# ScalarE writes one column into both PSUM banks of a projection ahead of its products, in batches 2 to 4

## Chip, cores and metric

The kernel runs on one core of one Trainium2 chip. A time is device microseconds (us) of one execution of the whole program; the kernel before takes 903.56 us (median of three runs, 902.72 to 904.33). The engines are PE (TensorE, matmuls) with its weight loads (PEld), DVE (VectorE), ACT (ScalarE), POOL (GpSimd) and SP (SyncE, which issues the transfers).

## What is computed

Four batches of a linear attention with random features, then two feed-forward blocks over all 2304 rows. Cut to what matters here:

```python
def phi(x):                                    # x: (4, 8, 576, 64), omega: (128, 64)
    proj = np.einsum('bhsd,md->bhsm', x, omega)
    sq = np.sum(x * x, axis=-1, keepdims=True) / 2.0
    h = proj - sq
    h = h - np.max(h, axis=-1, keepdims=True)
    return np.exp(h) / np.sqrt(m)
q_p, k_p = phi(q * scale), phi(k * scale)
kv = einsum('bhsm,bhsd->bhmd', k_p, v)         # and z = sum of k_p over s
out = einsum('bhsm,bhmd->bhsd', q_p, kv) / (einsum('bhsm,bhm->bhs', q_p, z)[..., None] + 1e-06)
h = x @ w_in;  x = (h * np.clip(h + 3.0, 0.0, 6.0) / 6.0) @ w_out      # block 1
h = x @ w2_in; y = (h / (1.0 + np.exp(-1.702 * h))) @ w2_out           # block 2
```

## The kernel before

**Stages.** The attention of batch 1 (`b` = 0 in the code) comes first, up to about 54 us of the profile. Then block 1 runs batch by batch over 16 chunks each (`emit_h`, `emit_o`), and the attention of the next batch (`b` = 1, 2, 3) is worked off step by step between its matmuls (`side`): the span from 54 to about 410 us. From there on block 1 of the last batch and block 2 (`h_pair`, `o_pair`) run without any attention. Chunks of `emit_o` follow those of `emit_h` two units later (`LAG`).

**The projection.** `PJ(h)` projects k and q of one head (512 of the 576 rows), `PL()` the remaining 64 rows of all heads of a batch. Both call `project` (lines 282 to 291): eight products of a 64-row stationary operand with omega (64 x 128), four for each half of the partitions. The half from partition 64 on writes the bank `ps[1]`, the other the bank `ps[0]`, and they alternate, `half` = 1 first. Each product is two matmul instructions in the profile, so a projection is 16. `behind(last)` fixes the order of the eight products among themselves, not that nothing else comes between them. `features` (lines 293 to 300) then takes the maximum of each bank on DVE (L295) and four exponentials of it on ACT (L297). A batch has 8 `PJ` and one `PL`; the three batches of the change have 27 projections.

**Banks.** PSUM has eight banks. Four belong to the pool `psp`, four to `acc`. From 54 us on `bank` hands out `psp` alone, because `emit_o` (L555) accumulates in the four of `acc`. The four of `psp` go round among the products of `emit_h` (L513), read by ACT L524 and DVE L525, the projections (two at a time), KV products (L347, L355), transposes (L369, L324, L433) and the numerators (L386).

**Order.** The program is laid out by a planner that runs through the text with a simulated clock. It gives every engine a fixed list of instructions; among those whose operands and bank are free by its reckoning, the one that stands earlier in the text goes first. A `behind(x)` block adds to an instruction only that it stands after `x` in the list of the same engine. On the chip each engine goes through its list in order and waits where a semaphore is not there yet. Banks are handed out in the order of the text.

**Lines the change and the steps touch:** L289 projection matmul; L295 maximum; L297 exponentials; L363 copy of the KV product; L374 copy of the transposed features; L524, L525, L529, L530 the gate of block 1; L213, L236, L252 conversion of weights and their sums; L513, L555, L856, L1008 the matmuls of the blocks.

Of the kernel before, what the change touches and what calls it, by code (L numbers as in the profile page):

```python
# [22 lines left out]
def performer_moe_kernel(  # L23
# [13 lines left out]
    nc = tc.nc  # L37
# [50 lines left out]
    three = const.tile([P, 1], F32, name="three")  # L88
# [20 lines left out]
    def bank(shape, name):  # L109
        n_ps[0] += 1  # L110
        if banks[0] == "acc" or banks[0] == "both" and n_ps[0] % 2:
            return acc.tile(shape, F32, tag="acc", name="acc")
        return psp.tile(shape, F32, tag="ps", name="ps")

    def behind(*ins):
        stack = ExitStack()
        for i in ins:
            if i is not None:
                stack.enter_context(tc.issue_after(i.ins))
        return stack  # L120
# [158 lines left out]
        nc.scalar.copy(hi, ps)  # L279
        nc.vector.tensor_tensor(out=lo, in0=ps, in1=hi.bitcast(F32), op=ALU.subtract)  # L280

    def project(a, ps):

        last = None
        for n in range(4):
            for half in (1, 0):
                rows = HALVES[half]
                with behind(last):
                    last = nc.tensor.matmul(  # L289
                        out=ps[half][:, n, :], lhsT=a(rows, n), rhs=omt[rows, :], start=True, stop=True  # L290
                    )

    def features(ps, e):
        mx = at.tile([P, 4], F32, tag="mx", bufs=4, name="mx")
        dve = nc.vector.reduce_max(mx, ps, axis=AX.X, negate=True)  # L295
        for r in range(4):
            act = nc.scalar.activation(  # L297
                out=e[:, r, :], in_=ps[:, r, :], func=AF.Exp, bias=mx[:, r:r + 1]
            )
        return act, dve  # L300

    class Att:
# [10 lines left out]
        def PL(self):  # L313
            a, self.vl = lqkv.pop(self.b)
            self.el = at.tile([P, 2 * NPAIR, M], F32, tag="el", name="el")
            ps = [bank([P, NPAIR, M], "ps") for _ in HALVES]
            project(lambda rows, i: a[rows, i, :], ps)
            for j, p in enumerate(ps):
                features(p, self.el[:, j * NPAIR:(j + 1) * NPAIR])

# [9 lines left out]
        def PJ(self, h):  # L330
            a = qkv[self.b, h // 2][0][:, h % 2]
            ps = [bank([P, R, M], "ps") for _ in HALVES]
            project(lambda rows, n: a[rows, n // 2, n % 2, :], ps)
            self.e[h] = at.tile([P, 2, R, M], F32, tag="e", bufs=2, name="e")
            for half, p in enumerate(ps):
                self.feat[h] = features(p, self.e[h][:, half])
# [347 lines left out]
    ps = bank([P, 4, P], "ps")  # L684
# [122 lines left out]
    for u in range(len(units) + LAG):  # L807
        while fetches and fetches[0][0] <= u + AHEAD:
            fetch_w(0, *fetches.pop(0)[1:])
        if u < len(units):  # L810
            n, c = units[u]
# [433 lines left out]
```

## Time and profile before

| | |
|---|---|
| median of three runs | 903.56 us |
| the profiled execution | 906.58 us |
| its span, first to last instruction | 904.8 us |
| mean granted TensorE clock | 0.998 of full speed |
| PE busy / weight loads busy | 98% / 84% of the span |
| DVE / ACT / POOL busy | 61% / 53% / 36% |
| instructions | 16525 |

Times in the rows are those of the profiled execution, from its first instruction on. Matmuls are pipelined: a matmul is shown with a duration longer than the distance to the next one, so the distance between two starts tells what it costs PE. A view by stretches gives busy time of each engine, the granted clock and the share of the transfer engines. A timeline merges neighbours of one line into one row, with their count; the number in brackets is idle time of the engine before the row, and what ended it.

### The profile page before, as it was taken

The numbers are of one execution on the slowest core, as the hardware profiler recorded it, in microseconds if no ns is written. First come the engines' busy times: TensorE is split into PE (matmuls) and PEld (weight loads), VectorE is DVE, ScalarE is ACT, GpSimd is POOL, SyncE is SP. The second block draws the span as 40 slices with busy tenths as digits, with TensorE's granted clock in tenths as the row PEclk, the third lists the DMA queues.
The fourth block names the chain that finished last, engine by engine and source line by source line (L and its number), as shares of the span: only waits on it lengthen the run. The fifth ranks groups of instructions, "written<-read, shape, count | busy, mean of one in ns | idle before, by whom it ended". The sixth has DMA issues, their size and how long they took to land.

```text
span 904.8 us, 16525 instructions
## 1 busy us (share of the span) xinstructions
PE 886.0 (98%) x6344; PEld 757.1 (84%) x6344; DVE 554.3 (61%) x952; ACT 478.0 (53%) x973; POOL 322.6 (36%) x257
## 2 busy tenths in 40 slices
PE   8899999999999999999999999999999999999998
PEld 6667777788788778878888888878999888899998
DVE  5887688473754736475573343666887343368785
ACT  5887677376664666656553343444545232245452
POOL 0122222044636565475673121877000243440000
PEclk9999999999999999999999999999999999999999
DMA  6677669698888987778857325999889644565562
GB/s 209 226 248 270 234 239 316 245 329 282 286 275 288 342 304 290 233 276 288 314 204 256 128 98 206 349 400 356 277 288 354 233 170 162 180 174 153 158 204 82
DMA packets 74416, 224.57 MB, mean 248 GB/s; under 512 B 7521, under 2 KB 13793, under 8 KB 74337
## 3 DMA queue, kind: packets, MB, share of 16 engines
q1 hardware_dynamic: 73872, 223.12, 71.1%
q8 instruction: 50, 0.82, 0.4%
q10 hardware_dynamic: 464, 0.39, 0.2%
q14 instruction: 30, 0.24, 0.1%
HBM read 160.57 MB, written 62.91 MB: 247 GB/s over the span
## 4 chain that ended last, share of the span: by engine, by line
PE 82%; DVE 8%; ACT 6%; issue 1%; POOL 1%; DMA 1%; DVEq 0%; SPq 0%; ACTq 0%; POOLq 0%
PE o L1008 19%; PE o L555 18%; PE ps L513 18%; PE h L856 16%; PE hl L873 3%; PE ps L289 2%; ACT e L297 2%; DVE w L236 2%; PE ps L386 1%; PE ps L347 1%; ACT wtop L213 1%; DVE mx L295 1%; DVE wtop L221 1%; PE ps L369 1%; DVE gs L530 1%
## 5 line engine op out<-in xcount | busy, mean ns | idle before, releaser
L513 PE MATMUL ps<-x,wss 128*128 128x512 f32 x768 | 195.5, 399 | 2.5 <-ACT el L297 1.1
L1008 PE MATMUL o<-wss,gs 128*128 128x256 f32 x1512 | 173.9, 277 | 0.2 <-DVE gs L977 0.2
L1008 PEld LDWEIGHTS o<-wss,gs 128*128 128x128 f32 x1512 | 173.4, 188 | 0.9 <-DVE gs L977 0.6
L513 PEld LDWEIGHTS ps<-x,wss 128*128 128x128 f32 x768 | 140.9, 189 | 35.0 <-ACT wss L239 3.1
L856 PE MATMUL h<-xo,wss 128*128 128x512 f32 x672 | 158.5, 391 | 0.9 <-DVE t L889 0.9
L856 PEld LDWEIGHTS h<-xo,wss 128*128 128x128 f32 x672 | 123.9, 188 | 27.5 <-DVE t L889 1.8
L228 POOL TENSOR_TENSOR w<-w,wpow 128x1024 f32<-128x1024 f32 x32 | 69.2, 2162 | 204.6 <-DVE wpow L225 166.7
L525 DVE SCALAR_TENSOR_TENSOR ga<-ga,ps 128x512 f32<-128x512 f32 x80 | 50.1, 632 | 121.1 <-ACT ga L524 121.1
L899 POOL TENSOR_TENSOR g<-g,c 128x512 f32<-128x512 f32 x48 | 64.7, 1349 | 164.0 <-ACT g L898 163.8
L976 ACT CAST gs<-g 128x512 fp32r<-128x512 f32 x112 | 69.6, 622 | 80.3 <-PE o L1008 49.3
L555 PE MATMUL o<-gs,wsh 128*128 128x512 f32 (+1 forms) x480 | 110.4, 374 | 1.2 <-ACT gs L529 1.0
L555 PE MATMUL o<-gs,wss 128*128 128x512 f32 (+1 forms) x480 | 109.5, 374 | 0.2 <-ACT gs L529 0.2
L253 POOL TENSOR_TENSOR wsn<-w,wsn 128x512 fp32r<-128x512 f32 x64 | 86.6, 1367 | 63.5 <-ACT wsn L252 63.5
L977 DVE TENSOR_TENSOR gs<-g,gs 128x512 fp32r<-128x512 f32 x112 | 79.9, 716 | 33.6 <-ACT gs L976 32.3
L524 ACT ACTIVATE ga<-ps,three 128x512 f32<-128x512 f32 x80 | 51.4, 650 | 86.5 <-PE ps L513 86.0
L555 PEld LDWEIGHTS o<-gs,wsh 128*128 128x128 f32 x480 | 82.2, 188 | 17.6 <-ACT gs L529 1.4
L555 PEld LDWEIGHTS o<-gs,wss 128*128 128x128 f32 x480 | 82.4, 188 | 15.8 <-ACT gs L529 0.4
L297 ACT ACTIVATE e<-ps,mx 128x128 f32<-128x128 f32 x220 | 61.1, 396 | 23.5 <-DVE mx L295 23.3
L530 DVE TENSOR_TENSOR gs<-ga,gs 128x512 fp32r<-128x512 f32 x80 | 62.5, 791 | 16.5 <-ACT gs L529 14.7
L898 ACT ACTIVATE g<-c 128x512 f32<-128x512 f32 x48 | 30.3, 632 | 60.2 <-DVE c L889 60.2
L529 ACT CAST gs<-ga 128x512 fp32r<-128x512 f32 x80 | 46.0, 580 | 27.8 <-DVE ga L525 27.4
L252 ACT CAST wsn<-w 128x512 fp32r<-128x512 f32 x64 | 38.3, 620 | 39.5 <-DVE w L236 13.2
(132 smaller groups left out, 1102.7 us busy)
## 6 DMA issues: line engine op xcount, KB each, us to landing
wss<-left SPq DMA_DIRECT2D x56, 512.0 KB, 3.9
wss<-ws0i SPq DMA_DIRECT2D x48, 512.0 KB, 4.9
wraw<-in_w_in_dram SPq DMA_DIRECT2D x32, 512.0 KB, 5.4
wraw<-in_w_out_dram SPq DMA_DIRECT2D x32, 512.0 KB, 6.3
left<-wsn SPq DMA_DIRECT2D x32, 512.0 KB, 3.7
wss<-ws0o SPq DMA_DIRECT2D x24, 512.0 KB, 4.6
ws0i<-wss SPq DMA_DIRECT2D x16, 512.0 KB, 3.3
wss<-sumsa SPq DMA_DIRECT2D x16, 512.0 KB, 3.5
```

The lines of the kernel that those rows point to most:

```text
L228: nc.gpsimd.tensor_tensor(out=w, in0=w, in1=q, op=ALU.mult)
L253: nc.gpsimd.tensor_tensor(out=s[:, :, 1], in0=t, in1=s[:, :, 0].bitcast(F32), op=ALU.subtract)
L297: act = nc.scalar.activation(out=e[:, r, :], in_=ps[:, r, :], func=AF.Exp, bias=mx[:, r:r + 1])
L513: nc.tensor.matmul(out=ps, lhsT=w[:, wi, kk, :], rhs=x[:, xi, kk, :], start=(m == 0), stop=(m == 3 * NK - 1),)
L524: nc.scalar.activation(out=g, in_=ps, func=AF.Relu, bias=three)
L530: gate[1] = nc.vector.tensor_tensor(out=s[:, 1, :], in0=g, in1=s[:, 0, :].bitcast(F32), op=ALU.subtract)
L555: nc.tensor.matmul(out=ps[:, e, :], lhsT=w[:, wi, cols], rhs=s[:, gi, :], start=(c == 0 and m == 0 and e == 0), stop=(c == NC - 1 and m == ...
L856: nc.tensor.matmul(out=ps, lhsT=s[:, wi, q, :], rhs=xop[q, op][:, xi], start=(first and m == 0), stop=(m == 5), skip_group_check=not first,)
L899: mul = eng.tensor_tensor(out=g, in0=g, in1=src, op=ALU.mult)
L976: split_ins[0] = nc.scalar.copy(hi, g)
L977: split_ins[1] = nc.vector.tensor_tensor(out=lo, in0=g, in1=hi.bitcast(F32), op=ALU.subtract)
L1008: last_row[0] = nc.tensor.matmul(out=out, lhsT=s[:, gi, d * P:(d + 1) * P], rhs=w[:, wi, :], start=(start and m == 0), stop=(stop and m == 2),
```

## The change

In batches 2 to 4 (`self.b > 0`) a projection begins with two copies on ACT: the constant column `three` (128 x 1) into the first column of `ps[0]`, then into that of `ps[1]`. Both columns are overwritten by the products. A product of either half writes the bank that its copy wrote and so follows it; as `half` = 1 comes first, and its copy stands second, the first product follows both. Of batch 1 nothing is changed.

```diff
-    def project(a, ps):
+    def project(a, ps, both=False):
 
         last = None
+        if both:
+            with behind(nc.scalar.copy(ps[0][:, 0, 0:1], three)):
+                nc.scalar.copy(ps[1][:, 0, 0:1], three)
         for n in range(4):
             for half in (1, 0):
                 rows = HALVES[half]
...
-            project(lambda rows, i: a[rows, i, :], ps)
+            project(lambda rows, i: a[rows, i, :], ps, self.b > 0)
...
-            project(lambda rows, n: a[rows, n // 2, n % 2, :], ps)
+            project(lambda rows, n: a[rows, n // 2, n % 2, :], ps, self.b > 0)
```

## Rows read from the trace of the kernel before

**Rows 1.** The page: busy us (share of the span) and instructions of each engine.

```profile
PE 886.0 (98%) x6344; PEld 757.1 (84%) x6344; DVE 554.3 (61%) x952; ACT 478.0 (53%) x973; POOL 322.6 (36%) x257
```

**Rows 2.** Busy time by stretch: length, then engines (x instructions), clock, transfers.

```profile
54.00:410.00 356.00, 351.90 (x2609) 279.05 (x2608) 223.07 (x405) 230.35 (x491) 152.64 (x118) 1.00 0.79 278
410.00:905.00 495.00, 489.58 (x3185) 443.62 (x3184) 292.76 (x456) 210.27 (x374) 161.78 (x128) 1.00 0.67 228
```

**Rows 3.** Waits of PE, 54 to 400 us: us in total, times, longest.

```profile
PE o L555 <- ACT gs L529: 1.1, 2, 1.0
PE ps L513 <- ACT el L297: 1.1, 1, 1.1
PE ps L289 <- DVE ga L525: 0.7, 1, 0.7
```

**Rows 4.** Line L289, 54 to 400 us: instructions, duration min/median/max, first and last start.

```profile
L289 PE MATMUL ps<-omt,qk x368: 272/272/373, 57.6 to 389.5; 64*128 64x128 f32 x184
...
L289 PE MATMUL ps<-omt,lqk x48: 272/272/373, 53.9 to 310.0; 64*128 64x128 f32 x48
```

**Rows 5.** Timeline of PE around 131 us: start us, us, what, count.

```profile
131.25 0.61 PE L513 MATMUL ps<-x,wss 128*128 128x512 f32 x2
131.79 1.16 PE L289 MATMUL ps<-omt,qk 64*128 64x128 f32 x16
132.88 1.43 PE L513 MATMUL ps<-x,wss 128*128 128x512 f32 x5
```

**Rows 6.** Timeline of PE, 82.9 to 87.5 us.

```profile
82.60 1.07 PE L513 MATMUL ps<-x,wss 128*128 128x512 f32 x4
83.60 0.48 PE L289 MATMUL ps<-omt,qk 64*128 64x128 f32 x2
84.02 2.11 PE L555 MATMUL o<-gs,wsh 128*128 128x512 f32 x8
86.06 1.16 PE L289 MATMUL ps<-omt,qk 64*128 64x128 f32 x14
87.14 0.73 PE L555 MATMUL o<-gs,wsh 128*128 128x512 f32 x2
```

**Rows 7.** Timeline of PE, 53.9 to 58 us.

```profile
53.94 0.48 PE L289 MATMUL ps<-omt,lqk 64*128 64x128 f32 x2
```

**Rows 8.** Timeline of PE, 387 to 390 us.

```profile
387.58 0.48 PE L289 MATMUL ps<-omt,qk 64*128 64x128 f32 x2
388.00 0.73 PE L555 MATMUL o<-gs,wss 128*128 128x512 f32 x2
...
389.75 0.44 PE L369 MATMUL ps<-ident,e 128*128 128x128 f32 x2
```

**Rows 9.** Timeline of PE, 202.2 to 204.5 us.

```profile
202.93 1.37 PE L289 MATMUL ps<-omt,qk 64*128 64x128 f32 x16
204.23 0.50 PE L513 MATMUL ps<-x,wss 128*128 128x512 f32 x1
```

**Rows 10.** Groups of ACT by form: busy us, mean ns of one; idle before.

```profile
L213 ACT ACTIVATE wtop<-wraw 128x1024 bf16<-128x1024 bf16 x32 | 36.6, 1149 | 0.0
...
L374 ACT COPY qpt<-ps 128x512 f32<-128x512 f32 x24 | 14.4, 598 | 5.6 <-PE ps L369 5.4
```

**Rows 11.** Line L363: copies of 128x65, duration min/median/max.

```profile
L363 ACT COPY kv<-ps x26: 189/216/294, 20.5 to 403.0; 128x65 f32<-128x65 f32 x26
```

**Rows 12.** Timelines of DVE and of PE, 311 to 318.5 us.

```profile
311.31 3.59 DVE L236 TENSOR_TENSOR w<-w,wtop 128x512 f32<-128x512 f32 x4
314.82 0.67 DVE L525 SCALAR_TENSOR_TENSOR ga<-ga,ps 128x512 f32<-128x512 f32 x1
...
315.55 1.16 PE L289 MATMUL ps<-omt,qk 64*128 64x128 f32 x14 [0.74 <-DVE ga L525]
```

**Rows 13.** Busy time by stretch behind these waits, columns as in the view above.

```profile
318.00:320.00 2.00, 2.00 (x6) 1.51 (x7) 0.58 (x1) 2.00 (x9) 1.92 (x3) 0.51 0.85 288
320.00:324.00 4.00, 4.00 (x18) 3.28 (x17) 0.69 (x1) 2.66 (x9) 3.69 (x6) 0.82 0.99 379
```

## The prediction

> **What bounds the kernel now.** I read the page first, then stretches, then the waits of PE, then single projections in the timeline. The page puts PE at 98% busy [rows 1]; since ends of matmuls are modelled, that alone proves little. By stretch, the one that the change touches, 54 to 410 us, has PE busy 351.90 of 356.00 us, ACT 230.35, DVE 223.07; behind it PE is at 489.58 of 495.00 [rows 2]. The waits decide: from 54 to 400 us the three largest waits of PE's matmuls are 1.1, 1.1 and 0.7 us [rows 3], under 4 us with the smaller ones. So PE almost never stands still here, and the stage gets shorter only if PE's list needs less time; behind 410 us PE is as full, and what is won earlier is passed on to the end.
>
> What PE's list loses shows in the timeline. Full matmuls of 512 columns start every 0.23 us: four in a row take 1.07 us and two 0.61, so (1.07 - 0.61) / 2 [rows 5, 6]. A projection in one piece is 16 instructions starting at 131.79, and the next matmul starts 1.09 us later [rows 5]. Between 54 and 400 us there are 368 + 48 = 416 such instructions, 26 projections [rows 4]; the 27th of batches 2 to 4 runs before 54 us. Nine of the 26 are cut: one product (2 instructions) goes ahead alone, then full matmuls, then the other 14. The nine start at 53.94, 83.60, 97.40, 188.03, 214.82, 238.87, 311.59, 338.16 and 387.58 us (the first, the last and the one that I work out stand in [rows 6 to 8]).
>
> **What a cut costs.** At 83.60 us the projection takes from 83.60 to 87.14, 3.54 us, with eight full matmuls in it: 3.54 - 8 x 0.23 = 1.70, against 1.09 in one piece, so 0.61 us [rows 5, 6]. At 387.58: 389.75 - 387.58 - 2 x 0.23 = 1.71, so 0.62 [rows 8]. Where it goes: the lone product takes 0.42 us up to the next start [rows 6], where in one piece two run side by side, and PE changes between 64-row and 128-row work four times instead of twice. I take 0.61 for each of nine, 5.5 us. A tenth, at 202.93, is in one piece, but 1.30 us from the next start, not 1.09, so 0.2 more [rows 9]. **In all 5.7 us of PE time, if no projection is cut any more.** I leave out an eleventh (57.6 us), whose first product ran beside the end of another projection.
>
> **Why the change takes the cuts away.** The list is the planner's: the first product needs only the bank `ps[1]`, so it is placed when that is free, and the next in the list is whatever is ready while `ps[0]` is still held. With the change the first product follows both writes, and the writes follow both releases. When it can go, the other seven can. The banks are handed out in the order of the text, so the writes overtake nobody, and the second bank comes when it came before; the full matmuls that stood inside the cut now stand ahead of the projection. The others, which ran in one piece, gain nothing.
>
> **What is added on ACT.** 27 x 2 = 54 writes of 128x1. No row shows one. A copy of 128x512 out of PSUM takes 0.598 us [rows 10], one of 128x65 0.216 (0.189 to 0.294) [rows 11]; the line through 0.598 and 0.216 gives 0.16 at one column. Bounds 0.16 to 0.29, and I take 0.20, near the smaller shape: 54 x 0.20 = 10.8 us (8.6 to 15.7). ACT has 356.00 - 230.35 = 126 us free in the stage [rows 2], so this lies beside other work. A gain is excluded for this term, as ACT did nothing of the kind before. The Trainium skill ("ScalarE: Activation LUTs", What ACT_TABLE_LOAD costs) states 186 ns + 0.833 ns per column for an ACTIVATE with immediate scale and bias, 0.187 us by estimate for one column; by that the 54 would be 10.1 us; no run here shows it yet.
>
> **What is added on the path.** Before, PE waited for the release itself: DVE's L525 starts at 314.82, takes 0.67, and PE starts at 315.55, 0.06 us after its end [rows 12]. Now release, write, PE: 0.20 + 0.06 at least, more where ACT is inside another instruction (up to 1.15, L213 [rows 10]), so 0.26 to 1.4 us later for each projection. The new wait sits in ACT's list; queued behind it are the reads L524 of PSUM, the casts L529, the exponentials L297 and the copies of weight sums L252, and for those DVE (L525, L530), the banks and finally PE wait. Cover: PE has matmuls of an earlier chunk (L555) at hand, as the cuts show (eight at 84.02). At the start of a batch the cover is thin: the only waits of a projection for a bank, and of L513 for exponentials, stand at 315 to 318 us [rows 3, 12]. I take 0.4 us for each of three batch starts (0.26, and a share of an instruction in progress), 1.2 us, and 1.0 for the other 24, one in eight of which finds no cover at some 0.35. Together 2.2 us; bounds 0 (all covered) and 27 x 1.4 = 38 (none). The lower end is much nearer, as the waits that PE has today show [rows 3].
>
> **A second edge of a stall.** After the waits at 315 to 318 the granted clock is 0.51 at 318 to 320 and 0.82 at 320 to 324, that is 1.2 GHz for a time, and 2.4 GHz again [rows 13]. Lost: 2 x 0.49 + 4 x 0.18 = 1.7 us. With the two waits (0.74 and 1.1 [rows 3, 12]) such an event costs 3.5 us. The changed list may lose this one or get others; I count none in the sum.
>
> **Sum.** -5.7 + 2.2 = -3.5 us. The profiled execution has 906.58 us (span 904.8), 3.0 above the median of the runs, 903.56; the sum is a difference within one execution, so 906.58 becomes 903.1, and the median **900.1 us**.
>
> **A rule that speaks against it.** In the stage the weight loads are busy 279.05 of 356.00 us, 78% [rows 2]. The Trainium skill ("Perfetto Trace Analysis", Identifying the Most-Contended Engine) says that matmul busy time is a poor measure and that headroom of TensorE is to be judged by the busy share of its weight loads. By that rule PE would have a fifth of the stage to spare, the switches would lie in this slack, and the time would stay at 903.6. The rows bear it out little: in gapless chunks the starts are 0.23 us apart, while PE waits for nobody [rows 3, 6].
>
> **Rivals.**
> 1. *The hand-over eats the gain*: 5.7 / 27 = 0.21 us exposed at each projection is enough, hardly more than one write. For it: ACT is busy 65% of the stage, so many a write finds ACT occupied. Against: PE's waits are few and L555 is mostly at hand. The same time results if PE's switches lie in slack. Time 903.6 (901.8 to 905.4), chance 0.18.
> 2. *Slower, by ACT's list*: a write whose bank is released late on the chip (as at 314.82, where L525 stood behind four L236 of 3.59 us in all [rows 12]) holds up ACT, and with it the gates and exponentials that free further banks; PE runs dry as at 315 to 318, clock included, at 3.5 us an event. One new event takes the 3.5 of the sum back, and beyond it the change loses; with four, 14.0 - 3.5 = +10.5, or 914; I take three, 10.5 - 3.5 = +7.0: 910.6. Against: today only one such event is left in three batch starts. Chance 0.18 (905.4 to 914).
> 3. *The planner still cuts*: something earlier in the text becomes ready inside a projection. The writes then come on top: +0 to +1.5 us, 904. Against: 17 of 26 were not cut. Chance 0.04.
> 4. *More than the sum*: the event at 315 to 318 us goes as well, as its first wait was for a bank of a cut projection: -5.7 - 3.5 + 2.2 = -7.0, or 896.6. Chance 0.10.
>
> **How the numbers follow.** Forecast 0.50 (896.5 to 901.7). About 0.2% (1.8 us) is what a measurement of this kernel can tell from no change. Faster by more: forecast and rival 4, 0.60. Within: rivals 1 and 3, 0.22. Slower by more: rival 2, 0.18. The range takes in rival 4 at its own value, rivals 1 and 3, and the lower part of rival 2: 896.0 to 907.0, which leaves out some 0.04 below and 0.13 above.
>
> **What the profile after would show.** Right: L289 in groups of 16 in one piece, about 1.1 us to the next start, at all 26 places, none with two instructions alone; 54 new ACT instructions of about 0.2 us; PE waits between 54 and 400 us for the new writes of 2 us or so; the last attention matmul, and everything behind it, about 4 us earlier, with the part behind 410 us as long as before. Wrong step "cuts": pieces of 2 and 14 are still there. Wrong step "cover": PE waits for the new line by more than 6 us in all, or L513 and L555 wait longer for L524, L529 and L297. Wrong step "PE is the bound": the cuts are gone and PE's stretches are no shorter. Beyond those, a list in quite another order, with PE idle at places that have nothing to do with projections, would make the forecast wrong.

## The result: 912.29 us, 1% slower

The changed kernel takes 912.29 us (median of five, 909.27 to 914.79), the kernel before, beside it, 903.11 (902.17 to 904.33): a ratio of 1.0098, 95% interval 1.0071 to 1.0125. The prediction was 900.1 us with a range up to 907.0; it had the sign wrong. Lines behind `project` are three higher than before: L289 is L292, L297 is L300, L524 to L530 are L527 to L533; the new writes are L286 and L287. One of the twelve executions of `z_best` below took 4930 us and is left out of its ratio.

**The page.** PE's busy time falls, its share falls as well, and ACT has 54 instructions more (line of the engines; compare [rows 1]).

```profile
PE 881.7 (97%) x6344; PEld 754.2 (83%) x6344; DVE 560.5 (62%) x952; ACT 482.7 (53%) x1027; POOL 321.2 (35%) x257
```

PE lost 4.3 us of work and the program became 5.7 us longer in span (910.5 against 904.8): PE now stands still for some 10 us more.

**The cuts are gone.** Timeline of PE where [rows 6] had a cut (start, duration, what, count):

```profile
85.83 0.73 PE L558 MATMUL o<-gs,wss 128*128 128x512 f32 x2
86.50 1.16 PE L292 MATMUL ps<-omt,qk 64*128 64x128 f32 x16
87.59 1.65 PE L558 MATMUL o<-gs,wsh 128*128 128x512 f32 x6
```

Sixteen in one piece, 1.09 us to the next start, as in [rows 5]; the trace shows the same at all 26 places between 54 and 400 us. The 27th projection, of the first head of batch 2, runs earlier and is not in one piece: eight instructions at 38.42 us and eight at 40.38.

**The writes are cheap.** The two lines, whole span: duration min/median/max in ns, first and last start.

```profile
L286 ACT COPY ps<-three x27: 150/163/235, 34.6 to 392.2; 128x1 f32<-128x1 f32 x27
...
L287 ACT COPY ps<-three x27: 149/163/223, 35.9 to 392.9; 128x1 f32<-128x1 f32 x27
```

**Where the time went.** I cut both traces at the same matmuls, the first L516 (before: L513) of a chunk: first head of batch 2; attention of batch 2 beside chunks 2 to 15; of batch 3; of batch 4; the rest. Busy time by stretch (columns as in [rows 2]), of the kernel after:

```profile
33.00:55.00 22.00, 16.07 (x171) 11.37 (x171) 18.22 (x45) 16.92 (x44) 4.27 (x2) 1.00 0.67 232
55.00:177.00 122.00, 117.65 (x848) 91.52 (x848) 92.23 (x180) 86.13 (x184) 27.90 (x13) 0.99 0.73 251
177.00:294.20 117.20, 115.63 (x889) 92.96 (x888) 68.39 (x113) 73.58 (x178) 57.00 (x47) 1.00 0.83 287
294.20:419.10 124.90, 119.12 (x905) 95.53 (x902) 69.95 (x113) 76.92 (x187) 70.06 (x63) 1.00 0.80 284
419.10:910.50 491.40, 486.20 (x3157) 440.70 (x3155) 291.46 (x455) 208.08 (x368) 158.12 (x124) 1.00 0.67 228
```

The same of a second profiled execution of the kernel before, run later (`x_before`, span 902.2 us), which lacks the fall of the clock of [rows 13] and is therefore the better base:

```profile
33.10:53.20 20.10, 16.55 (x170) 11.65 (x170) 17.50 (x43) 15.66 (x40) 4.26 (x2) 1.00 0.70 233
53.20:171.60 118.40, 116.51 (x844) 90.10 (x844) 89.07 (x180) 85.77 (x169) 27.88 (x13) 1.00 0.77 264
171.60:289.40 117.80, 117.66 (x893) 94.73 (x892) 67.80 (x114) 72.28 (x161) 56.93 (x47) 1.00 0.83 285
289.40:411.50 122.10, 120.38 (x906) 96.35 (x903) 68.20 (x113) 75.04 (x169) 71.17 (x63) 1.00 0.82 290
411.50:902.20 490.70, 485.59 (x3157) 440.93 (x3155) 292.06 (x455) 207.91 (x368) 158.67 (x124) 1.00 0.67 228
```

From these cuts to the hundredth: +1.86 in the first stretch, +3.67 beside batch 2, -0.61 beside batch 3, +2.83 beside batch 4, +0.7 in the rest. The counts of PE in the rows have to be read first: 848 against 844 beside batch 2, 889 against 893 beside batch 3. Four full matmuls of `emit_o` (L558, before L555) that ran just behind the cut between these two stretches now run just ahead of it. At 0.227 us each they carry 0.9 us from batch 3 to batch 2. For the same work batch 2 is 2.8 us longer, and batch 3 is not shorter but 0.3 longer.

The difference then splits into four parts. *Waits*: where the profile shows PE idle ahead of a matmul, the distance between the two starts, less the usual one behind a matmul of that form (0.227 us at 512 columns, 0.105 for a projection's; medians of `x_before`). *Clock*: what the matmuls at 1.2 GHz took more. *Moved*: the four matmuls. *Rest*: what is left; the cuts that are gone are the known part of it.

| stretch | waits of PE | clock | moved | rest | measured |
|---|---|---|---|---|---|
| first head of batch 2 | +2.4 | | | -0.5 | +1.86 |
| batch 2 | +2.8 | +1.7 | +0.9 | -1.8 | +3.67 |
| batch 3 | +1.6 | | -0.9 | -1.3 | -0.61 |
| batch 4 | +4.4 | | | -1.5 | +2.83 |

So of the 5.7 us that the prediction took off, 4.6 show beside batches 2 to 4, and 11.2 us of new waits and 1.7 us of a slower clock stand against all that was won. Waits of PE, 54 to 410 us (us in total, times, longest; compare [rows 3]):

```profile
PE ps L516 <- ACT wss L239: 3.9, 4, 1.6
PE ps L292 <- ACT ps L287: 3.2, 3, 2.5
PE ps L516 <- issue: 1.6, 1, 1.6
PE ps L516 <- ACT el L300: 1.2, 1, 1.2
PE ps L516 <- ACT kv L366: 1.0, 1, 1.0
```

Only the second row is the new wait. The first and the third are waits that the prediction does not contain. In the first, block 1's matmuls wait for a cast of weights (L239). For the third, at 358.34 us, the profile shows no release; DVE's read L424 of a bank ends at 358.24, so it may be a bank.

**The wait for the write, in full.** PE at the start of batch 4:

```profile
318.30 1.16 PE L292 MATMUL ps<-omt,lqk 64*128 64x128 f32 x16
321.96 0.71 PE L292 MATMUL ps<-omt,qk 64*128 64x128 f32 x8 [2.50 <-ACT ps L287]
```

DVE's read that frees the second bank is L528, 319.94 to 320.62:

```profile
319.94 0.68 DVE L528 SCALAR_TENSOR_TENSOR ga<-ga,ps 128x512 f32<-128x512 f32 x1
```

And ACT, which has to hand it over:

```profile
319.98 0.16 ACT L286 COPY ps<-three 128x1 f32<-128x1 f32 x1
320.70 0.62 ACT L532 CAST gs<-ga 128x512 fp32r<-128x512 f32 x1 [0.57 <-DVE ga L528]
321.23 0.61 ACT L252 CAST wsn<-w 128x512 fp32r<-128x512 f32 x1
321.75 0.15 ACT L287 COPY ps<-three 128x1 f32<-128x1 f32 x1
```

The bank is free at 320.62. In ACT's list the cast L532, which waits for the same L528, and L252 come first; the write, 0.15 us long, ends at 321.90, and PE starts at 321.96, 1.34 us after the release. Before it was 0.06 us [rows 12]. The price of the hand-over is what stands ahead of the write, not the write. PE's wait is longer, 2.50 us, because it begins ahead of the release: PE has nothing else at hand. In `x_before` sixteen full matmuls stand between the start of batch 4's first projection and the main part of the second:

```profile
310.22 1.43 PE L555 MATMUL o<-gs,wss 128*128 128x512 f32 x5
311.58 0.48 PE L289 MATMUL ps<-omt,qk 64*128 64x128 f32 x2
311.99 2.81 PE L555 MATMUL o<-gs,wsh 128*128 128x512 f32 x11
```

After, fifteen of them stand ahead of both projections, one behind, and none between the two. So 1.34 us of this wait are the hand-over, and the 1.16 before it are for want of cover.

**The wait beside batch 2.** PE, some 131 us:

```profile
129.65 0.66 PE L436 MATMUL ps<-ident,xt 128*128 128x128 f32 x4
131.93 0.73 PE L516 MATMUL ps<-x,wss 128*128 128x512 f32 x2 [1.63 <-ACT wss L239]
```

No write stands near: the last ones of ACT before it are at 115.77 and 116.37 us. ACT's list ten microseconds earlier, after:

```profile
119.03 0.62 ACT L532 CAST gs<-ga 128x512 fp32r<-128x512 f32 x1 [0.76 <-DVE ga L528]
121.82 2.18 ACT L300 ACTIVATE e<-ps,mx 128x128 f32<-128x128 f32 x8 [2.17 <-DVE mx L298]
123.84 0.67 ACT L239 CAST wss<-w 128x512 fp32r<-128x512 f32 x1
...
125.35 1.20 ACT L213 ACTIVATE wtop<-wraw 128x1024 bf16<-128x1024 bf16 x1
```

and in `x_before`, where the same head's exponentials come earlier against the casts and their wait is shorter:

```profile
117.55 2.18 ACT L297 ACTIVATE e<-ps,mx 128x128 f32<-128x128 f32 x8 [0.98 <-DVE mx L295]
...
120.13 0.68 ACT L239 CAST wss<-w 128x512 fp32r<-128x512 f32 x1
...
121.16 1.21 ACT L213 ACTIVATE wtop<-wraw 128x1024 bf16<-128x1024 bf16 x1
```

After, ACT stands still for 2.17 us with the weight casts queued behind the exponentials; the conversion of weights (L213, L236, L239), which feeds block 1 just in time, falls behind. The trace follows it to PE: L213 starts at 125.35, DVE works on its result from 126.58 to 128.20, POOL's L228 runs from 128.37 to 130.50, DVE's L236 starts at 130.53, the cast L239 at 131.26, PE at 131.93. From its first to its last L213 in this stretch, thirteen instructions, it takes 55.3 to 158.8 us, before 54.8 to 153.4. Then PE waits for a cast, and the clock falls. Busy time by stretch, after:

```profile
130.00:133.20 3.20, 1.16 (x9) 0.48 (x9) 2.67 (x5) 2.70 (x6) 0.50 (x1) 1.00 0.29 119
133.20:136.60 3.40, 3.40 (x22) 2.80 (x23) 3.40 (x9) 2.15 (x5) 0.13 (x1) 0.50 0.59 163
```

PE is busy 1.16 of 3.20 us, and the granted clock is then 0.50 (1.2 of 2.4 GHz) for 3.4 us: another 1.7 us.

### The profile page after: what moved, and what is told of

The parts are those of the page before. It is cut to its first block, busy times and chain, and to the rows that moved or that the text cites. A ratio compares the mean times of both kernels' runs of the same rounds, so it can differ in the third digit from the quotient of the medians.

```text
span 910.5 us, 16611 instructions
## 1 busy us (share of the span) xinstructions
PE 881.7 (97%) x6344; PEld 754.2 (83%) x6344; DVE 560.5 (62%) x952; ACT 482.7 (53%) x1027; POOL 321.2 (35%) x257
## 4 chain that ended last, share of the span: by engine, by line
PE 78%; DVE 7%; ACT 7%; DMA 3%; issue 2%; POOL 2%; SPq 0%; DVEq 0%; ACTq 0%; POOLq 0%
PE o L1011 19%; PE ps L516 18%; PE o L558 17%; PE h L859 14%; PE hl L876 2%; PE ps L292 2%; PE ps L389 2%; DVE w L236 2%; ACT e L300 2%; PE ps L372 1%; ACT wtop L213 1%; DVE mx L298 1%; PE ps L350 1%; DVE gs L533 1%; ACT w L215 1%
## 5 line engine op out<-in xcount | busy, mean ns | idle before, releaser
L516 PE MATMUL ps<-x,wss 128*128 128x512 f32 x768 | 195.0, 399 | 9.0 <-ACT wss L239 3.9
L516 PEld LDWEIGHTS ps<-x,wss 128*128 128x128 f32 x768 | 140.3, 189 | 42.7 <-ACT wss L239 5.4
L228 POOL TENSOR_TENSOR w<-w,wpow 128x1024 f32<-128x1024 f32 x32 | 69.0, 2155 | 209.8 <-DVE wpow L225 144.5
L528 DVE SCALAR_TENSOR_TENSOR ga<-ga,ps 128x512 f32<-128x512 f32 x80 | 50.0, 632 | 109.3 <-ACT ga L527 109.2
L558 PE MATMUL o<-gs,wsh 128*128 128x512 f32 (+1 forms) x480 | 109.2, 373 | 1.1 <-DVE gs L533 0.9
L558 PE MATMUL o<-gs,wss 128*128 128x512 f32 (+1 forms) x480 | 107.9, 373 | 0.0
L527 ACT ACTIVATE ga<-ps,three 128x512 f32<-128x512 f32 x80 | 51.1, 647 | 86.3 <-PE ps L516 86.2
L558 PEld LDWEIGHTS o<-gs,wsh 128*128 128x128 f32 x480 | 82.3, 188 | 17.3 <-DVE gs L533 2.1
L558 PEld LDWEIGHTS o<-gs,wss 128*128 128x128 f32 x480 | 82.5, 188 | 15.5
L533 DVE TENSOR_TENSOR gs<-ga,gs 128x512 fp32r<-128x512 f32 x80 | 66.6, 842 | 19.4 <-ACT gs L532 17.3
L300 ACT ACTIVATE e<-ps,mx 128x128 f32<-128x128 f32 x220 | 61.4, 398 | 23.2 <-DVE mx L298 23.2
L532 ACT CAST gs<-ga 128x512 fp32r<-128x512 f32 x80 | 45.8, 577 | 28.3 <-DVE ga L528 28.2
L252 ACT CAST wsn<-w 128x512 fp32r<-128x512 f32 x64 | 38.3, 621 | 37.8 <-DVE w L236 9.6
```

The lines of the kernel that those rows point to most:

```text
L228: nc.gpsimd.tensor_tensor(out=w, in0=w, in1=q, op=ALU.mult)
L300: act = nc.scalar.activation(out=e[:, r, :], in_=ps[:, r, :], func=AF.Exp, bias=mx[:, r:r + 1])
L516: nc.tensor.matmul(out=ps, lhsT=w[:, wi, kk, :], rhs=x[:, xi, kk, :], start=(m == 0), stop=(m == 3 * NK - 1),)
L527: nc.scalar.activation(out=g, in_=ps, func=AF.Relu, bias=three)
L533: gate[1] = nc.vector.tensor_tensor(out=s[:, 1, :], in0=g, in1=s[:, 0, :].bitcast(F32), op=ALU.subtract)
L558: nc.tensor.matmul(out=ps[:, e, :], lhsT=w[:, wi, cols], rhs=s[:, gi, :], start=(c == 0 and m == 0 and e == 0), stop=(c == NC - 1 and m == ...
```

## The experiments

Theories at the start: (1) **hand-over**: PE is late because it waits for ACT, at the places where a write stands late in ACT's list; (2) **another list**: any edit changes the planner's order, and the new order has gaps of its own, whatever is inserted. Stage lengths below are cut as above, in us; the base is 20.14 / 118.34 / 117.85 / 122.06 (`x_before`: first head, batch 2, batch 3, batch 4). Ratios are to the kernel before on the same chip, with 95% intervals; stages are of one profiled execution of each kernel. Where batch 2 is edited, the four matmuls of the table above are in its stage and not in that of batch 3, which makes 0.9 us; `z_b2early` alone has them where they were.

**One part alone: batch 2, or batches 3 and 4.**

```diff
-            project(lambda rows, i: a[rows, i, :], ps, self.b > 0)
+            project(lambda rows, i: a[rows, i, :], ps, self.b == 1)
```

(`w_b2`; the same in `PJ`; `w_b34` has `self.b > 1`.)

> The two writes in batch 2 alone (9 of 27 projections). Theory 1 (ScalarE's list is what PE ends up waiting for, where ScalarE also converts the weights of block 1, and that is the stage of batch 2 only): nearly the whole loss, +4 to +6 us, 908 to 909, with waits of L513 for the conversion casts L239. Theory 2 (waiting for both banks makes every projection late, batch by batch alike): a third of the loss, +3 us, 906. Theory 3 (no cause but a reshuffled list): no relation to the count, anything from -3 to +6.

> The two writes in batches 3 and 4 alone (18 of 27 projections). Theory 1: the stage of batch 2 is as before, the other two as in the changed kernel (-0.65 and +0.85 there): 903 to 904, no difference. Theory 2: two thirds of the loss, +6 us, 909. Theory 3: anything from -3 to +6, and the stages of batches 3 and 4 need not look like those of the changed kernel.

Measured: `w_b2` 909.06 us, 1.0058 [1.0043, 1.0074]; stages 21.98 / 122.02 / 117.12 / 121.76. `w_b34` 906.24, 1.0033 [1.0021, 1.0044]; 20.14 / 118.20 / 116.98 / 124.80. The losses lie where the writes are, and they nearly add up: +5.5 and +2.7, or 8.2, against +9.2 for all. Batch 2 has the larger part of it, batch 4 nearly all of the rest.

**Another engine, one write, or no write.** `w_dve` lets DVE write both columns; `w_one` writes `ps[0]` alone and makes the first product wait for that write too; `x_pe` has no write at all: a product of zeros on PE goes to `ps[0]` first, so that PE itself waits for both banks.

```diff
-            with behind(nc.scalar.copy(ps[0][:, 0, 0:1], three)):
-                nc.scalar.copy(ps[1][:, 0, 0:1], three)
+            with behind(nc.vector.tensor_copy(ps[0][:, 0, 0:1], three)):
+                nc.vector.tensor_copy(ps[1][:, 0, 0:1], three)
```

```diff
-            with behind(nc.scalar.copy(ps[0][:, 0, 0:1], three)):
-                nc.scalar.copy(ps[1][:, 0, 0:1], three)
+            w = nc.scalar.copy(ps[0][:, 0, 0:1], three)
```

```diff
-            with behind(nc.scalar.copy(ps[0][:, 0, 0:1], three)):
-                nc.scalar.copy(ps[1][:, 0, 0:1], three)
+            last = nc.tensor.matmul(out=ps[0][:, 0, :], lhsT=zero_r, rhs=zero_r, start=True, stop=True)
```

> The same 54 writes, on VectorE in place of ScalarE, so the bank hand-over stays and ScalarE's list is as before. Theory 1: most of the loss goes, 902 to 906. Theory 2: the same loss, 911 to 913. Theory 3: anything.

> One write on ScalarE a projection (into the bank of the second product), and a wait of the first product for it; the first product takes its own bank from its last reader. Both banks still stand ready before the first product. Theory 1: half the writes, about half the loss, 906 to 909. Theory 2: the whole loss, 911 to 913. Theory 3: anything.

> Both banks before the first product, without a second engine: PE itself multiplies zeros (128x128) into the second product's bank ahead of the first product, in 128-row mode; the later product overwrites it. 27 more matmuls of 0.11 us and some weight load: +3 to +4 us of PE time, and the cuts' 5.2 us gone. Theory 1 (ScalarE's list and the hand-over): 901 to 903. Theory 2 in the form that waiting for both banks itself makes the projections late: as the changed kernel or worse, 910 to 914. Theory 3: 900 to 912.

Measured: `w_dve` 913.54, 1.0106 [1.0089, 1.0124]; 22.13 / 121.73 / 116.50 / 128.21. `w_one` 906.97, 1.0041 [1.0026, 1.0056]; 22.11 / 119.95 / 115.31 / 124.05. `x_pe` 906.32, 1.0020 [1.0007, 1.0033]; 20.21 / 119.30 / 116.42 / 124.79. It is not ACT as such: DVE does it as badly. PE alone, with no hand-over, does not lose beside batch 2: its +0.96 us there are the four moved matmuls, and eight products of zeros stand in the stage besides. Beside batch 4 it still loses, with a wait of 1.57 us for the bank at 314.91 and a fall of the clock behind it. `w_one` has almost no wait beside batch 3 (busy time by stretch, whole stage):

```profile
174.40:289.70 115.30, 114.93 (x890) 93.03 (x889) 66.87 (x113) 72.41 (x169) 56.82 (x47) 1.00 0.81 285
```

117.85 - 115.31 = 2.5 us, but its 890 instructions against 893 show that the four moved matmuls are missing here: the gain for the same work is 1.6. It is made of 2.0, which is what the prediction's step gives (3 x 0.61 + 0.2), less 0.4 of waits. At the start of batch 4 `w_one` settles what `after` leaves mixed. Its first product waits there for the reader of its own bank (L534, before L525), with no write behind that release, and PE still waits as long:

```profile
315.64 1.59 PE L292 MATMUL ps<-omt,qk 64*128 64x128 f32 x16 [2.40 <-DVE ga L534]
```

Only two full matmuls stand between this projection and the one ahead of it. An order without cover leaves PE as long a wait here as cover and hand-over together do in the changed kernel.

**ACT's time without the dependence.** Before, with a tiny copy on ACT behind the exponentials of each bank in batches 2 to 4, tied to no bank, and with no matmul behind it: `x_load` into a new tile, `y_load` onto itself, `z_load3` three of them per bank (162 in all). `x_before` is the kernel before again.

```diff
+        if extra:
+            nc.scalar.copy(mx[:, 0:1], mx[:, 0:1])
```

> The kernel before once more, for a second profile: 902 to 905 us. All theories expect the same list; what differs from the first profile (the fall of the clock at 318 us among it) is what executions differ by.

> Before, with two 1-column copies on ScalarE for each projection of batches 2 to 4 behind its exponentials, into a scratch column: ScalarE's added time without any part in the banks; the cuts stay. Theory 1 (ScalarE's occupied time makes PE wait): the stalls of the changed kernel that are not for the writes themselves, 10.1 - 3.2 = 6.9 us, 910. Theory 2 (the projection's start waits for a hand-over through another engine and for both banks): 903 to 904.5. Theory 3 (a reshuffled list alone): 900 to 910 without a rule.

> As the run with two scratch copies a projection, but the copies go from and to the first column of mx, so that no tile is added and no address moves. In that run 5 us of the 7 lay behind 545 us, where no attention runs, with full matmuls 0.232 us apart in place of 0.227. Loop theory: the time on ScalarE alone, 54 x 0.16 us, lengthens the stage of batch 2 by 1 to 3 us and leaves the rest: 905 to 907. Hand-over theory: 903 to 904.

> Before, with three in-place copies of one column (mx) behind the exponentials of each bank, 162 in all, 26 us of ScalarE in place of 8.6: no part in the banks. ScalarE's time as the cause: three times the effect of the run with 54, +6 to +7 us in the stage of batch 2 and +5 to +8 in all, 909 to 912. List luck: no relation to the dose, 900 to 910.

Measured: `x_before` one execution of 904.01. `x_load` 911.37, 1.0082 [1.0066, 1.0098], but that is no clean test: its new tile moved 27 others by 32 bytes each, and 5 us of its loss lie in block 2, which has neither projections nor copies: 359.88 against 354.73. `y_load`, without the tile: 906.00, 1.0024 [1.0015, 1.0034]; 20.16 / 120.69 / 116.89 / 124.01, block 2 at 354.99. `z_load3` 907.17, 1.0040 [1.0027, 1.0054]; 21.09 / 120.04 / 117.20 / 122.66. Up to the end of batch 2 one copy per bank costs +2.4 us and three cost +2.65, 0.9 of either for the moved matmuls: it does not go by ACT's time. These kernels still have nearly all of their cuts, and no hand-over; so a loss beside batch 2 needs none.

**The loop of the weights.** As the conversion of weights fell behind beside batch 2, I gave its first buffer a second copy: in the kernel before (`y_wtb`), the changed one (`y_wta`) and the one with one write (`y_wto`).

```diff
-tag=f"wtop{l and c % 2}"
+tag=f"wtop{c % 2}"
```

> Before, with the weight halves wtop of block 1 in two buffers in turn (the tag that block 2 uses already, so no memory moves). Loop theory (the stage of batch 2 is paced by one conversion after the other: L213 may overwrite wtop only when both L236 of the chunk before have read it, 8.22 us a chunk): the period falls to PE's own need, the stage gets 1 to 3 us shorter, 901 to 903. Theory of ScalarE's occupied time alone: no change, 903 to 904. Theory 3 (list luck): 898 to 910.

> The changed kernel with wtop in two buffers. Loop theory: the writes no longer lengthen the pace of the stage of batch 2 and its cuts are a gain: its +3.7 us become -1 to -2 against the form without writes; left is the loss at the start of batch 4 (+2.8) and before the stage (+1.9): 904 to 907. Theory of ScalarE's occupied time alone: still +8 to +9, 911 to 913.

> One write a projection, with wtop in two buffers. Loop theory: 900 to 903, the stages of batches 2 and 3 both at 115 to 117 us. Theory of ScalarE's occupied time alone: 907.

Measured: 916.75, 1.0148 [1.0130, 1.0165]; 926.27, 1.0252 [1.0232, 1.0272]; 917.79, 1.0153 [1.0131, 1.0174]. The theory fell. The loop did get quicker (7.37 us from one L213 to the next in `y_wtb`, 8.22 before), but the weights were then ready 9 to 23 us ahead of need instead of 0 to 3 (first cast of a chunk, from the second chunk of the stage on). PE waited for exponentials and gates instead, which fits that ACT and DVE had done the weights in place of them. Waits of PE in `y_wtb`, 54 to 190 us:

```profile
PE ps L369 <- ACT e L297: 3.8, 2, 2.3
PE ps L513 <- DVE ga L525: 2.0, 3, 1.6
```

**The start of a batch.** `z_b34h` is `w_b34` without the writes of the first two projections of batch 4 (`PL` and the first `PJ`); `z_ah` is the changed kernel without these two in every batch.

```diff
-            project(lambda rows, n: a[rows, n // 2, n % 2, :], ps, self.b > 0)
+            project(lambda rows, n: a[rows, n // 2, n % 2, :], ps, self.b > 0 and h > 0)
```

> The two writes in batches 3 and 4 without PL and the first PJ of batch 4. Hand-over at the start of a batch: the 2.5 us wait for the second write is gone, the stage of batch 4 takes 121 to 123 us in place of 124.8, in all 902 to 904 against 906.2 with them. If the loss of that stage is list luck or the number of writes: 905 to 907.

> The changed kernel without writes for PL and the first PJ of each batch (21 of 27 projections keep them). Hand-over at the starts: the 1.9 us ahead of the stage of batch 2 and the 2.8 us of the stage of batch 4 are gone, the stage of batch 2 keeps 2 to 4: 905 to 908. Otherwise 910 to 913.

Measured: `z_b34h` 904.24, 1.0005 [0.9990, 1.0020]; 20.36 / 118.30 / 117.00 / 122.65. `z_ah` 907.79, 1.0045 [1.0030, 1.0060]; 20.15 / 121.69 / 116.34 / 123.80. Waits of PE, 290 to 411 us, with the two projections' writes (`w_b34`):

```profile
PE ps L292 <- ACT ps L287: 2.7, 2, 2.5
PE ps L516 <- issue: 1.7, 1, 1.7
```

and without them (`z_b34h`):

```profile
PE ps L516 <- issue: 1.6, 1, 1.6
PE o L558 <- ACT gs L532: 0.9, 1, 0.9
```

The 2.5 us are gone and so are 2.0 us of the time (906.24 to 904.24): the condition on these two projections is the cause of that part. It brings the hand-over and the order without cover together; `w_one` shows that the order alone can make as long a wait. `z_ah` shows the same for the first head of batch 2 (22.00 back to 20.15). What stays in `z_ah` is batch 4, at +1.7 us with another wait of 2.0 (L558 for the cast L532), and batch 2, at +3.35 us, with the same longest wait as the changed kernel (waits of PE, 54 to 175 us):

```profile
PE ps L516 <- ACT wss L239: 2.0, 2, 1.6
```

**The place beside batch 2.** `z_b2early` has the two writes in batch 2 alone, and only in `PL` and heads 1 to 4, whose projections stand ahead of the long wait.

```diff
-            project(lambda rows, n: a[rows, n // 2, n % 2, :], ps, self.b > 0)
+            project(lambda rows, n: a[rows, n // 2, n % 2, :], ps, self.b == 1 and 0 < h < 5)
```

> The two writes in batch 2 for PL and the heads 1 to 4 alone, not for the first PJ and not for the heads 5 to 7. If the loss of the stage of batch 2 is the one place at 118 to 134 us: the early cuts stay a gain, the stage ends at 116 to 117.5 us in place of 118.3, in all 901.5 to 903. If the writes cost by their number or by ScalarE's time: 905 to 907 (half of +5.2 and more). List luck: 900 to 909.

Measured: 908.57, 1.0056 [1.0039, 1.0073]; 20.32 / 121.66 / 117.91 / 122.30. The place is not it either: the wait for the cast is gone, another one is there (waits of PE, 54 to 175 us),

```profile
PE ps L372 <- DVE ga L528: 1.9, 1, 1.9
```

and the clock falls behind that one (stretches of `z_b2early`):

```profile
136.00:139.20 3.20, 1.24 (x20) 0.86 (x20) 3.20 (x8) 3.20 (x8) 0.00 (x0) 1.00 0.37 150
139.20:142.60 3.40, 3.21 (x8) 2.56 (x9) 2.85 (x7) 3.22 (x8) 0.38 (x1) 0.54 0.70 228
```

**The gain without the losses.** One write, kept away from the places that lost: `x_one3` in batch 3 alone, `z_one34h` in batch 3 and behind the first two projections of batch 4, `z_best` in batch 3 and as in `z_b2early`.

```diff
-            project(lambda rows, i: a[rows, i, :], ps, self.b > 0)
+            project(lambda rows, i: a[rows, i, :], ps, self.b == 2)
```

> One write a projection, in batch 3 alone, where the form with one write had no stall and took 115.3 us against 117.1 to 117.9. The cuts of that stage go, nothing else changes: theories 1 and 2 901 to 902 (-1.5 to -2.2). Theory 3: 900 to 907.

> The version that these causes point to: one write a projection, in batches 3 and 4 alone, without PL and the first PJ of batch 4. The stage of batch 2 as before; batch 3 at 115.3 to 116.3 us (-1.5 to -2.5), batch 4 at 120.5 to 122 (-1.5 to 0): 899.5 to 902. List luck: 899 to 906.

> One write a projection, for PL and the heads 1 to 4 of batch 2 and all of batch 3. Place theory: both stages gain, 899.5 to 902. By number or time: 904 to 906. List luck: 899 to 909.

Measured: `x_one3` 903.10, 0.9988 [0.9976, 1.0001]; 20.39 / 118.32 / 116.32 / 121.85. `z_one34h` 902.98, 0.9990 [0.9979, 1.0001]; batch 3 at 116.17, batch 4 at 123.76 with a fall of the clock in it. `z_best` 904.94, 1.0015 [1.0004, 1.0027]; batch 2 at 119.84. The first two win 1.5 to 1.7 us beside batch 3 in the profile, with the same matmuls in the stage as before (`x_one3`):

```profile
171.10:287.40 116.30, 115.88 (x894) 93.73 (x892) 67.38 (x114) 73.06 (x170) 57.14 (x47) 1.00 0.82 286
```

Over the whole time their intervals touch no change, and both stay above the range that was expected of them.

**All together.** Beside batch 2 the kernels that leave its list alone (`w_b34`, `x_one3`, `z_b34h`, `z_one34h`) take 118.20 to 118.32 us, as before. All that change anything in it, and keep the buffers of the weights, take 119.30 to 122.02. Without the moved matmuls `x_pe`, with a product on PE, is where the kernel before is; those with writes on ACT or DVE, one or two, or with copies that no matmul waits for, are at +0.6 (`z_best`) to +3.3 (`z_b2early`).

## Why the prediction was wrong, point by point

**What bounds the kernel: half right.** Time of PE taken away does come back, but only where the new list brings few waits: 1.5 us beside batch 3 in `x_one3`, 1.6 in `w_one` for the same work. There the rule of the Trainium skill that I had weighed ("Perfetto Trace Analysis", Identifying the Most-Contended Engine: headroom of TensorE by its share of the peak rate, MFU, and by the busy share of its weight loads) would, by the loads, have given nothing: they are busy 94.73 of 117.80 us in that stage before, 80%. The measurement goes against it. What I missed: few waits of PE do not mean slack on ACT and DVE. Before, weights were ready 0 to 3 us ahead of need beside batch 2; that left little room for a list that does the conversion later.

**Cuts: right, their size a little high.** All nine are gone. The rest column shows 1.8, 1.3 and 1.5 us for the three stages, 4.6 where I took 5.7; beside batch 3 `x_one3` and `w_one` show 2.0. One sentence of that step did not hold everywhere: at 86.50 us the eight full matmuls that stood inside the cut now stand behind the projection. At the start of batch 4 they do stand ahead, but ahead of two projections, and nothing is left between these to cover a wait.

**Cost of a write: right.** 0.16 us where I took 0.20 and had a line at 0.16 at hand; 27 + 27 of them. The Trainium skill ("ScalarE: Activation LUTs", What ACT_TABLE_LOAD costs) gives 0.187 by estimate; measured are 0.163.

**Cover: too small, and for the wrong reason.** "Together 2.2 us." The direct wait was not far off: PE waited 3.2 us for the writes between 54 and 410 us, 2.5 of them at the start of batch 4. That was one of the three batch starts for which I took 0.4 each, worked out from the write and a share of one instruction in progress. The trace shows that the list counts, not the instruction in progress: two instructions of 0.62 and 0.61 us stood ahead of the write, the first of them waiting for the very release that was to be handed over; and half of the wait came before the release, with no cover. I had named that (the write queued behind others, up to 1.4 us) and then priced it as if a random instant of ACT were met. By its own sign (more than 6 us for the new line) this step would have passed; the larger loss lies elsewhere.

**"I count none in the sum": the step that failed.** For stalls elsewhere I had counted nothing, as if the rest of the list stayed. It did not: 11.2 us of waits came, of which some 3.2 are for the writes, and 1.7 us of a slower clock. The largest events are at 130 us (waits of 1.63 and 0.42 and the clock, near the 3.5 that I had priced), at 319 (2.50, without the clock) and at 356 us (1.65, without the clock).

**Rival 2 came nearest**: three events, 910.6 us, at a chance of 0.18. So its number is right by luck: its mechanism, a write held up in ACT, is shown at 319 us alone, and there for 1.34 of 2.50 us. At 130 us the exponentials wait for DVE's maximum, with no write in between, and the copies that no matmul waits for cause a loss beside batch 2 too. The last sentence on what would make the forecast wrong, a list in another order with PE idle at places that have nothing to do with projections, is what happened; it should have been a rival with a price, and with most of the chance.

**Rivals 1, 3 and 4**: the hand-over did not eat the gain evenly, and more than the gain was lost (rival 1 out); the planner cuts none of the 26 any more (rival 3 out); the event at 315 to 318 us did not go, it moved to 319 (rival 4 out).

**What stays open.** Which property of the list makes the loss beside batch 2. Shown: it needs no hand-over, does not grow in step with the number of copies, is not tied to ACT or to the later heads, does not come with the product on PE, and is not cured by a second buffer for the weights. That the order of ACT and DVE before happens to be a good one, from which almost any step leads to a worse one, fits all of it, but it is argued, not shown. For the +1.86 us in the first head of batch 2, `z_ah` shows that the first two projections' writes make it. The longest part is its last wait: PE starts at 54.98 us after 1.40 us for the cast L239, 0.06 in `x_before`. How the writes delay that cast was not followed.

## What to carry to other kernels

A wait that is moved from one engine to another costs what stands ahead of it in the second engine's list: read that list at the place, and do not take an average instant. Where PE is full and the lists of two other engines feed it just in time, an edit that changes a planned order must be priced with one or two stall events of the size that the trace already shows, and not at nothing. Before two stretches are compared, count the matmuls in both: four that crossed a cut looked like a gain beside batch 3. And an experiment that adds a tile may move others; compare a stage that the edit does not touch, before its time is believed.

## What of the hardware was unexpected

**Addresses.** In `x_load` a tile of one column moved 27 tensors in SBUF, and the matmuls of block 2, untouched by the edit, became slower. Costliest groups of PE by form, 550 to 800 us (busy us, mean ns of one, idle before), `x_load`:

```profile
L859 PE MATMUL h<-xo,wss 128*128 128x512 f32 x644 | 154.0, 394 | 1.2 <-DVE t L892 0.5 <-DMA wss<-sumsd 0.4 <-ACT p L911 0.2
```

and `x_before`:

```profile
L856 PE MATMUL h<-xo,wss 128*128 128x512 f32 x650 | 152.6, 390 | 0.8 <-DVE t L889 0.5 <-DMA wss<-sumsd 0.3
```

Their starts are 0.232 us apart instead of 0.227, and block 2 takes 359.88 us against 354.73. That the addresses are the reason is inferred from the comparison with `y_load` (354.99), which differs by the tile and the target of the copies alone.

**The clock.** Of two profiled executions of the kernel before, one has a stretch at 1.2 GHz [rows 13], the other has none, at the same list. `x_before` has the longer of the two waits ahead of it as well, 1.11 us. In the traces of the experiments nearly every fall follows waits of PE of 1.0 to 2.5 us, and not every such wait is followed by one: after the wait of 2.50 us at 319 us in the changed kernel the clock stays at 2.4 GHz (stretches of after, the wait and what follows).

```profile
319.00:321.90 2.90, 0.46 (x10) 0.27 (x6) 2.16 (x4) 2.07 (x6) 1.27 (x1) 1.00 1.02 412
321.90:325.50 3.60, 3.54 (x27) 3.00 (x28) 2.56 (x5) 2.82 (x12) 3.42 (x4) 1.00 1.03 408
```
